# Score bounds as rows of the query tile, and gate logits as a column of the value projections

## The chip, the cores and the metric

The kernel runs on one core of a Trainium2 chip. Its five engines run their own instruction streams side by side: TensorE (PE, matrix products, with the weight loads shown apart as PEld), VectorE (DVE), ScalarE (ACT), GpSimd (POOL) and SyncE (SP, which here only issues DMAs). The metric is the device time of one execution in microseconds, as the median of several runs. The kernel before took 780.24 us, the median of three runs between 780.03 and 782.4.

## The reference

One layer of 2048 tokens by 512 features: attention with 32 heads of 16 features, a gated feed-forward network (FFN), and a sigmoid gate for each token that mixes the two. All arrays are bf16.

```python
x = A_x                                              # 1 x 2048 x 512
g = sigmoid((x * gate_w).sum(-1, keepdims=True))
q, k, v = split((x @ wqkv), 3, heads=32)             # Dh = 16
p = softmax(einsum("bhqd,bhkd->bhqk", q, k) * 16 ** -0.5)
a = concat_heads(p @ v) @ wo
b = (silu(x @ w_gate) * (x @ w_up)) @ w_down         # 512 -> 1792 -> 512
return g * a + (1 - g) * b
```

Softmax divides by a sum, so any number may be subtracted from a row's scores first. The kernel subtracts an upper bound of the row's scores instead of their maximum: for query q and head h, the sum over the 16 features d of |q_d| times the largest |k_d| of any key.

## The kernel before

**Tiling.** Queries go in four blocks of 512 (`qb`), heads in eight groups of four (`g`), keys in sixteen tiles of 128 (`kt`). A *unit* is a pair (qb, g); there are 32 of them, with group 0 of all four blocks first. A unit has sixteen *slots*, one for each key tile, so 512 slots in all, and every deadline in the code counts in slots. In a slot, PE makes the scores of four heads, 128 keys by 512 queries each; they are exponentiated, and PE multiplies them by the values (`vaug`, with a column of ones that gives the denominator) into the unit's `o_ps`.

**Layout of the score product.** A head has 32 partitions of the key tile `kaug` and of the query tiles `qx` and `q1`: the four heads of a group fill 128. In the kernel before, row 0 of the 32 is the bound (a one in `kaug`, minus the bound in the query tile), rows 1 to 16 the features, and the rest is zero in the query tile. `kaug` is filled with ones before the keys land. Some scores are made with 64 rows, two heads together; then the query tile's other plane holds zeros for the other head.

**Two ways to an exponential.** ACT exponentiates two heads' scores in one instruction (`e_t` from `s_t`, 128x1024, line 166), so a slot costs it two. Or DVE builds the slot: four conversions `c_t` from `d_t` (128x512 each, from PSUM, one for each head), which are the exponential's bits to first order, and then either three shifted copies of 128x2048 (`copy`, four approximations that the value product adds up, so that PE does four value products instead of one) or two bit operations and a product (`bits` and `product`, two value products). `kaug` and `wd_t` are used as homes for such tiles too, which is why the profile has rows like `kaug` from `d_t`.

**The planner.** All of this is ordered when the program is built. Every PE, ACT and DVE instruction goes out in the order in which the code calls it. `Plan` keeps an account of each engine's time: `spend` charges PE, `later(cost, f)` puts an instruction on a list for DVE with its cost, `ACT_US` is an exponential's cost and `MUL_US` that of the product in `product`. `v_unit` gives DVE a slot of the current or the next unit if DVE's account ends early enough before ACT would reach it; otherwise ACT gets it. Three PSUM banks (`m_tile`, `m_free`) serve projections, FFN products and `d_t`.

Side work is in chains (`pace.add(pieces, release, deadline, after, gap)`): projections, FFN products, output products. A chain starts at its release slot once the chains in `after` are done, and the one with the nearest deadline goes first. `need` forces chains at a slot; `q_of` says which chain must be done before DVE may take slots of a unit.

**The parts that the change touches.**

- `k_pieces` projects the keys of eight heads (b = 0 to 3) into `kst` and sends them to `kaug` by DMA. `k_bound` reduces |k| over all keys to `kb` (one number for each of 128 features), and multiplies a selection matrix `bsel` by it into `kneg` (128x8).
- `q_pieces` projects 512 queries of eight heads, copies them to `qst`, sends them to the query tiles in transfers of 16 rows, and puts |q| into `aq`.
- `bound_pieces` is a chain of its own: one product of `kneg` and `aq` into the bank `bp` (eight rows), an eviction to `bq`, four transfers into rows 0 of the query tiles. It follows `q_pieces` and `k_bound` with a gap of two slots.
- Group 0 has a path of its own (`q0_pieces`, `kneg0`), which stays as it is, with its bound in row 0.
- `v_pieces` projects the values of 128 keys for the 28 heads of groups 1 to 7: sixteen products of 128 by 448 columns (columns 64 to 511 of `wv`), evicted to `vaug`. Columns 0 to 63 (group 0) are read by `v0` and `v0_pieces` alone, earlier.
- `gate_pieces` makes the gate logits of two token tiles: eight products of one column each into `glog`, and a clamp to +-40 into `ge`. `gate_end` then makes the gate from all sixteen. `gw_col` is `gate_w` as a column, loaded in `late_loads` at slot 28.

SP issues every load and transfer in one queue in program order (the first small weights go through ACT's). GpSimd works in the first 11 us only.

Of the kernel before, what the change touches and what calls it, by code (L numbers as in the profile page):

```python
# [9 lines left out]
ALU = mybir.AluOpType  # L10
# [69 lines left out]
def kernel(  # L80
# [44 lines left out]
    SHIFTS = (25.0, 56.0, 94.0)  # L125
    EXP_A = 128.0 * inv_sqrt_dh * math.log2(math.e)
    EXP_B = {4: 128.0 * (127.0 - math.log2(5.372947814979324)), 2: 128.0 * (127.0 - math.log2(1.5015118813815151))}
    MUL_US = 1.2
    TINY = 1e-37
    AHEAD = 1  # L130
    SPARE = 0.5


# [28 lines left out]
    def mm(*args, **kw):  # L162
        return ordered(nc.tensor.matmul(*args, **kw))  # L163
# [42 lines left out]
    wo_l = big.tile([P, 2, D], BF16, name="wo_l")  # L206

    def late_loads():
        queue.dma_start(out=gw_col[:], in_=gate_w.rearrange("(dc p) -> p dc", p=P))
        queue.dma_start(out=wo_t[:], in_=A_wo.rearrange("(b p) d -> p b d", p=P))  # L210
        for i in range(2):
            for j in range(4):
                h = H - 8 + 4 * i + j
                queue.dma_start(out=wo_l[32 * j + 1:32 * j + 1 + DH, i, :], in_=A_wo[h * DH:(h + 1) * DH, :])
# [41 lines left out]
    for g in (1, 2):  # L256
# [9 lines left out]
    nc.gpsimd.memset(  # L266
        vaug[:, :, 0:G * 4 * VC].rearrange("p t (h c) -> p t h c", c=VC)[:, :, :, 0:1], 1.0)

    pidx = const.tile([P, 1], F32, name="pidx")
    nc.gpsimd.iota(pidx[:], pattern=[[0, 1]], base=0, channel_multiplier=1,  # L270
                   allow_small_or_imprecise_dtypes=True)
    bsel = const.tile([P, 8], BF16, name="bsel")
    lo_t = const.tile([P, 8], F32, name="lo_t")
    for h in range(8):
        c = 2 * (h % 4) + h // 4
        nc.gpsimd.memset(lo_t[:, c:c + 1], float(DH * h))
    far_t = const.tile([P, 8], F32, name="far_t")
    nc.gpsimd.memset(wo_l[:], 0.0)
    sbc_t = const.tile([P, P], BF16, name="sbc_t")
    nc.gpsimd.memset(sbc_t[:], 0.0)  # L280
# [6 lines left out]
        nc.gpsimd.memset(sel_t[32 * j:32 * j + 1, j:j + 1], 1.0)  # L287

    kb = const.tile([P, NB], F32, name="kb")
    kneg = const.tile([P, NB, 8], BF16, name="kneg")  # L290
    gval = const.tile([P, KT], F32, name="gval")
    omg = const.tile([P, KT], F32, name="omg")
    ge = const.tile([P, KT], F32, name="ge")
# [154 lines left out]
    def k_pieces(b, tb):  # L448

        def end(t, p):  # L450
            vec.tensor_copy(out=kst[b][:, t * QBW:(t + 1) * QBW], in_=p[:, :])
            m_free(p, plan.dve)
            if t == QB - 1:
                for hh in range(8):
                    g, j = 2 * b + hh // 4, hh % 4
                    if g > 0:
                        queue.dma_start(out=kaug[32 * j + 1:32 * j + 1 + DH, g, :],
                                          in_=kst[b][DH * hh:DH * (hh + 1), :])

        def lhs(dc):  # L460
            if dc == 0 and tb == 0:
                kst[b] = (on_t[1], bblk)[b == 1][:, :, :].rearrange("p b q -> p (b q)")
            return wqk[:, dc, D + P * b:D + P * (b + 1)]
        return columns(DC, "kp", lhs, lambda dc: xT[:, dc, tb * QBW:(tb + 1) * QBW],
                       lambda p: later(0.6, lambda: end(tb, p)))

    def k_bound(b):
        vec.tensor_reduce(out=kb[:, b:b + 1], in_=kst[b][:, :], axis=AX.X, op=ALU.max, apply_absolute_value=True)
        vec.tensor_scalar(out=kneg[:, b, :], in0=bsel[:, :], scalar1=kb[:, b:b + 1],
                          scalar2=None, op0=ALU.mult)  # L470

    def v0(t0):

# [33 lines left out]
    def v_pieces(tt):  # L507

        def end(p):
            dst = vaug[:, tt, 4 * VC:G * 4 * VC].rearrange("p (h c) -> p h c", c=VC)[:, :, 1:1 + DH]  # L510
            vec.tensor_copy(out=dst, in_=p[:, 64:D].rearrange("p (h c) -> p h c", c=DH))
            m_free(p, plan.dve)
        return columns(DC, "vp", lambda dc: xT[:, dc, tt * P:(tt + 1) * P], lambda dc: wv[:, dc, 64:D],
                       lambda p: later(0.54, lambda: end(p)), c0=64)

# [4 lines left out]
    for g in range(5, G):  # L522
# [1 line left out]

    q0 = [(qx[1][:, :, :, :], on_t[0][:, :, :].rearrange("p (v i) q -> p v i q", v=2))[qb // 2][:, :, qb % 2, :]
          for qb in range(QB)]
    aqs = {}

    def get_q(qb, g):
        return q1 if g == 1 else qx[(qb * (NB - 1) + g // 2 - 1) % 2][:, :, g % 2, :]  # L530
# [1 line left out]
    def q_pieces(qb, b):  # L532
        def landed(p):
            me = plan.chain
            later(0.6, lambda: end(p, me), key=("q", b))

        def end(p, me):
            qst = work.tile([P, QBW], BF16, tag="qst", name="qst")
            vec.tensor_copy(out=qst[:, :], in_=p[:, :])
            m_free(p, plan.dve)  # L540
            for hh in range(8):
                gg, j = hh // 4, hh % 4
                if (b, gg) != (0, 0):
                    queue.dma_start(out=get_q(qb, 2 * b + gg)[32 * j + 1:32 * j + 1 + DH, j % 2, :],
                                      in_=qst[DH * hh:DH * (hh + 1), :])

            def mag():
                aq = work.tile([P, QBW], BF16, tag="aq", name="aq", bufs=4)
                vec.tensor_scalar(out=aq[:, :].bitcast(U16), in0=qst[:, :].bitcast(U16),
                                  scalar1=0x7FFF, scalar2=None, op0=ALU.bitwise_and)  # L550
                aqs[(qb, b)] = aq
            plan.chain = me
            later(0.21, mag, plan.dve, ("q", b))
        return columns(DC, "qp", lambda dc: wqk[:, dc, P * b:P * (b + 1)],
                       lambda dc: xT[:, dc, qb * QBW:(qb + 1) * QBW], landed)
# [29 lines left out]
    def variants(p, to, q, more=()):  # L585
# [10 lines left out]
        later(0.4, select, key=key)  # L596
        for cost, f in more:
            later(cost, f, key=key)

    def bound_pieces(qb, b):  # L600

        st = {}

        def f():
            st["p"] = m_tile("bp")
            mm(st["p"][0:8, :], lhsT=kneg[:, b, :], rhs=aqs[(qb, b)][:, :], start=True, stop=True,
               tile_position=(0, 0))
            spend("C", 1)
            later(0.6, end)

        def end():
            bq = work.tile([8, QBW], BF16, tag="bq", name="bq")
            vec.tensor_copy(out=bq[:, :], in_=st["p"][0:8, :])
            m_free(st["p"], plan.dve)
            for j in range(4):
                if b == 0:
                    queue.dma_start(out=q1[32 * j:32 * j + 1, j % 2, :], in_=bq[2 * j + 1:2 * j + 2, :])
                else:
                    t = qx[(qb * (NB - 1) + b - 1) % 2]
                    queue.dma_start(out=t[32 * j:32 * j + 1, j % 2, :, :], in_=bq[2 * j:2 * j + 2, :])  # L620
        return [(1, f, True)]


    def gate_pieces(t0):
        def f():
            gp = m_tile("glog")
            for t in (t0, t0 + 1):
                for dc in range(DC):
                    mm(gp[:, t:t + 1], lhsT=xT[:, dc, t * P:(t + 1) * P],
                       rhs=gw_col[:, dc:dc + 1], start=(dc == 0), stop=(dc == DC - 1))  # L630
            spend("F", 2)

            def end():
                vec.tensor_scalar(out=ge[:, t0:t0 + 2], in0=gp[:, t0:t0 + 2], scalar1=-40.0, scalar2=40.0,
                                  op0=ALU.max, op1=ALU.min)
                m_free(gp, plan.dve)
            later(0.15, end)
        return [(0.7, f, True, "F", None)]

    def gate_end():  # L640
        act(out=ge[:, :], in_=ge[:, :], func=ACT.Exp, scale=-1.0)
# [507 lines left out]
    for g in (3, 4):  # L1149
        ones_rows(vec, g)  # L1150

    vec.tensor_scalar(out=lo_t[:], in0=lo_t[:], scalar1=pidx[:, 0:1], scalar2=None, op0=ALU.subtract)
    vec.tensor_scalar(out=far_t[:], in0=lo_t[:], scalar1=-float(DH) + 0.5, scalar2=-1.0,
                            op0=ALU.is_gt, op1=ALU.mult)
    vec.scalar_tensor_tensor(out=bsel[:, :], in0=lo_t[:], scalar=0.5, in1=far_t[:],
                                   op0=ALU.is_lt, op1=ALU.mult)
    plan.act = plan.pe
    plan.dve = plan.pe + 3.9

# [50 lines left out]
    need[9] = [v_late]  # L1210
    need[14] = [parts]
    q_of[0] = again
    v_rest = [pace.add(v_pieces(tt), 2, int(12 + 3 * tt)) for tt in range(KT)]

    def v_of(n):

# [12 lines left out]
    for qb in range(QB):  # L1229
        for b in range(NB):  # L1230
# [15 lines left out]
                rel = UNIT.index((qb - 1, 6)) * KT + 1 if qb else 0  # L1246
            else:
                rel = UNIT.index((qb, 2 * b - 2)) * KT + 1 if (qb, b) != (0, 2) else UNIT.index((0, 2)) * KT + 1
            q = pace.add(q_pieces(qb, b), rel, d - 25)
            bc = pace.add(bound_pieces(qb, b), rel, d - 22, [q] + after, 2)  # L1250
            need.setdefault(d - 12, []).append(bc)
            for g in {max(2 * b, 1), 2 * b + 1}:
                q_of[UNIT.index((qb, g))] = bc
    gates = [pace.add(gate_pieces(2 * i), 36 + 7 * i, 44 + 7 * i) for i in range(KT // 2)]
    gates = [pace.add([(0.2, gate_end, False)], 40, 106, gates)]
    turned = pace.add([(1, turn_odds, True, "F", None)], 40, 130, gates, 2)
    need.setdefault(160, []).append(turned)

# [118 lines left out]
    def begin(n):  # L1377
        plan.slot = n
        for c in need.get(n, []):
            force(c)  # L1380
        if n == 28:
            late_loads()
        i = n - (QB + 1) * KT - 8
        if 0 <= i < 2 * FC and i % 4 == 0:
            wd_load(i // 2)
        for f in at.pop(n, []):
            f()
        pace.begin_slot(n)
# [246 lines left out]
```

## Time and profile before

| what | value |
|---|---|
| median of three runs | 780.24 us |
| the profiled execution | 780.74 us |
| its span, first to last instruction | 778.8 us |
| granted TensorE clock, mean | 0.999 |
| first exponential starts, last one starts | 13.16 us, 769.69 us |
| `bq` from `bp`, 8x512, 16 times, DVE | 10.8 us busy, 673 ns each |
| `aq` from `qst`, 16 times, DVE | 4.6 us busy, 285 ns each |
| `ge` from `glog`, 8 times, DVE | 1.1 us busy, 151 ns each |
| `kneg` from `bsel` and `kb`, 4 times, DVE | 0.9 us busy, 229 ns each |
| `vaug` from `vp`, 128x448, 16 times, DVE | 9.9 us busy, 618 ns each |
| `bp`, 16 products, PE | 6.1 us busy, 379 ns each |
| `glog`, 64 products of one column, PE | 2.7 us busy, 165 ns each |
| loads and transfers | 32.63 MB, 42 GB/s over the span |

A group's *busy* time counts the time in which at least one of its instructions ran, and *mean* the duration of one. Instructions of one engine overlap (the next starts while the last results of the one before are still on their way), so a duration is longer than the step from one start to the next; where an engine is full, the step is the price. A timeline row merges neighbours of one kind: start, length, engine and line, operation, output and inputs, count, and in brackets the idle time before and what ended it. Since most instructions go through a helper, lines 163, 166 and 175 stand for nearly all of PE, ACT and DVE, and one reads by tile names.

### The profile page before, as it was taken

The page shows a single profiled execution, that of the slowest core. Times are in us where ns is not written, and L with a number is a line of the kernel's source. Part 1 is how long each engine was busy: PE and PEld are TensorE (multiplying, and loading weights), DVE is VectorE, ACT ScalarE, POOL GpSimd, SP SyncE. Part 2 cuts the span into 40 slices and gives each one's busy share as a digit, 9 for nine tenths or more (in the row PEclk, how much of TensorE's full clock was granted, in tenths as well). Part 3 has the DMA queues.
Part 4 walks back from the last instruction along what each step waited for, and adds up shares of the span by engine and source line. Part 5 has one row for each costly group of instructions (what it writes and reads, how often), then busy time and mean ns, then how long its engine had stood idle before and what let it go on. Part 6 is the DMA issues. An engine that isn't in the chain of part 4 may idle for free.

```text
span 778.8 us, 21608 instructions
## 1 busy us (share of the span) xinstructions
PE 740.7 (95%) x8877; PEld 223.6 (29%) x8877; DVE 725.5 (93%) x1162; ACT 764.5 (98%) x863; POOL 11.0 (1%) x34
## 2 busy tenths in 40 slices
PE   8999999999999999999999999989999989999997
PEld 3322333322222222232222222222222322222222
DVE  7799999899889999999999999999999999999994
ACT  5999999999999999999999999999999999999996
POOL 5000000000000000000000000000000000000000
PEclk9999999999999999999999999999999999999999
DMA  8002103134110112220100131211001222100001
GB/s 189 2 5 49 29 20 79 50 99 94 43 32 8 27 37 62 51 53 20 32 15 19 31 94 26 66 28 34 13 20 27 60 66 45 46 12 12 15 29 35
DMA packets 88138, 32.63 MB, mean 42 GB/s; under 512 B 74304, under 2 KB 87592, under 8 KB 88040
## 3 DMA queue, kind: packets, MB, share of 16 engines
q1 hardware_dynamic: 86312, 30.93, 16.5%
q8 instruction: 69, 1.13, 0.6%
q10 hardware_dynamic: 1728, 0.33, 0.2%
q14 instruction: 29, 0.24, 0.1%
HBM read 21.55 MB, written 2.35 MB: 31 GB/s over the span
## 4 chain that ended last, share of the span: by engine, by line
ACT 56%; PE 24%; issue 12%; DVE 7%; ACTq 0%; DVEq 0%
ACT e_t L166 53%; PE s_t L163 9%; PE o_ps L163 6%; PE gu L163 5%; DVE c_t L175 4%; ACT th L166 3%; PE qp L163 1%; PE dps L163 1%; DVE mt L175 1%; PE warm L163 1%; PE vp L163 1%; PE kp L163 1%; DVE gs L175 0%; PE ops L163 0%; DVE kaug L175 0%
## 5 line engine op out<-in xcount | busy, mean ns | idle before, releaser
L166 ACT ACTIVATE e_t<-s_t 128x1024 bf16<-128x1024 f32 x794 | 743.7, 1147 | 0.9 <-PE s_t L163 0.8
L175 DVE TENSOR_SCALAR c_t<-d_t 128x512 uint16<-128x512 f32 x404 | 267.8, 683 | 17.7 <-PE d_t L163 17.0
L163 PE MATMUL s_t<-qx,kaug 32*128 32x512 bf16 (+1 forms) x1252 | 244.3, 382 | 21.7 <-ACT e_t L166 19.6
L163 PEld LDWEIGHTS <-kaug 32*128 32x128 bf16 (+1 forms) x2048 | 97.9, 91 | 339.4 <-issue 334.6
L163 PE MATMUL o_ps<-e_t,vaug 128*32 128x512 bf16 x1588 | 154.9, 386 | 0.0
L175 DVE TENSOR_SCALAR c_t<-c_t 128x2048 uint16<-128x2048 uint16 x193 | 129.9, 685 | 1.1
L163 PE MATMUL d_t<-qx,kaug 32*128 32x512 bf16 x380 | 128.5, 384 | 0.0
L163 PE MATMUL o_ps<-c_t,vaug 128*32 128x512 bf16 x1028 | 97.8, 385 | 0.6 <-DVE osb L175 0.6
L163 PEld LDWEIGHTS <-vaug 128*32 128x32 bf16 x2800 | 59.5, 94 | 100.3 <-issue 94.2
L163 PE MATMUL gu<-xT,wg 128*32 128x512 bf16 x896 | 73.0, 384 | 0.0
L175 DVE TENSOR_TENSOR c_t<-c_t 128x2048 bf16<-128x2048 bf16 x59 | 71.7, 1215 | 0.0
L163 PE MATMUL gu<-xT,wu 128*32 128x512 bf16 x896 | 68.3, 382 | 0.1
L163 PE MATMUL ops<-wd_t,mt 128*32 128x512 bf16 x672 | 57.1, 382 | 0.0
L163 PE MATMUL s_t<-q,kaug 32*128 32x512 bf16 (+1 forms) x204 | 39.8, 382 | 6.0 <-ACT e_t L166 5.1
L175 DVE SCALAR_TENSOR_TENSOR gs<-th,gu 128x512 bf16<-128x512 bf16 x56 | 38.2, 682 | 3.4 <-ACT th L166 3.0
L175 DVE SCALAR_TENSOR_TENSOR mt<-gs,gu 128x512 bf16<-128x512 bf16 x56 | 38.2, 682 | 3.2 <-PE gu L163 1.5
L166 ACT ACTIVATE th<-gu 128x512 bf16<-128x512 f32 x56 | 40.9, 731 | 0.0
L175 DVE TENSOR_SCALAR kaug<-d_t 128x512 uint16<-128x512 f32 x52 | 34.8, 682 | 1.5 <-PE d_t L163 1.2
L163 PEld LDWEIGHTS <-mt 128*32 128x32 bf16 (+1 forms) x1037 | 24.1, 95 | 27.5 <-issue 21.6
L163 PEld LDWEIGHTS <-wu 128*32 128x32 bf16 x896 | 19.5, 95 | 24.1 <-issue 15.2
L163 PEld LDWEIGHTS <-wg 128*32 128x32 bf16 x896 | 17.4, 94 | 24.3 <-issue 21.8
L175 DVE TENSOR_SCALAR kaug<-c_t 128x2048 uint16<-128x2048 uint16 x35 | 24.0, 686 | 0.3
(149 smaller groups left out, 449.0 us busy)
## 6 DMA issues: line engine op xcount, KB each, us to landing
wg<-in_B_w_gate_dram SPq DMA_DIRECT2D x56, 128.0 KB
wu<-in_B_w_up_dram SPq DMA_DIRECT2D x56, 128.0 KB
on<-osb SPq DMA_DIRECT2D x120, 16.0 KB
rb<-rr SPq DMA_DIRECT2D x15, 128.0 KB
wd_t<-in_B_w_down_dram SPq DMA_DIRECT2D x7, 256.0 KB
qx<-qst SPq DMA_DIRECT2D x96, 16.0 KB
out_dram<-o_t SPq DMA_DIRECT2D x12, 128.0 KB
kaug<-on SPq DMA_DIRECT2D x20, 64.0 KB
```

The lines of the kernel that those rows point to most:

```text
L163: return ordered(nc.tensor.matmul(*args, **kw))
L166: ordered(nc.scalar.activation(*args, **kw))
L175: return lambda *a, **kw: ordered(f(*a, **kw))
```

## The change

The bound is no longer multiplied out. The query tile gets, beside the 16 rows of q, 16 rows of -|q_d| times `kb`, and `kaug` holds ones there, so that the score product itself adds the bound up. Rows 0 to 15 of a head are the features now and rows 16 to 31 the bound (group 0 keeps row 0). `aq` is q with its sign bit set, weighed by `kb` in place, and sent by the same transfers of 16 rows as q. `bound_pieces`, `bsel`, `lo_t`, `far_t`, `pidx` and `kneg` are gone; `q_pieces` waits for `k_bound` itself, and is due at `QLEAD` = 24 slots before use.

The gate vector is loaded at slot 3 and copied into column 63 of `wv`, which group 0's value products have read by then; each value projection takes 449 columns from column 63 on, and its first output column is the gate logit of its 128 tokens. `gate_pieces` is gone; the value projections wait for the copy, and their deadlines are two slots later. `MUL_US`, the planner's cost of the product, goes from 1.2 to 1.135.

```diff
-    MUL_US = 1.2
+    MUL_US = 1.135
+    QLEAD = 24
...
-        queue.dma_start(out=gw_col[:], in_=gate_w.rearrange("(dc p) -> p dc", p=P))
...
-                        queue.dma_start(out=kaug[32 * j + 1:32 * j + 1 + DH, g, :],
-                                          in_=kst[b][DH * hh:DH * (hh + 1), :])
+                        queue.dma_start(out=kaug[32 * j:32 * j + DH, g, :], in_=kst[b][DH * hh:DH * (hh + 1), :])
...
-        vec.tensor_scalar(out=kneg[:, b, :], in0=bsel[:, :], scalar1=kb[:, b:b + 1],
-                          scalar2=None, op0=ALU.mult)
...
         def end(p):
             dst = vaug[:, tt, 4 * VC:G * 4 * VC].rearrange("p (h c) -> p h c", c=VC)[:, :, 1:1 + DH]
+            vec.tensor_scalar(out=ge[:, tt:tt + 1], in0=p[:, 63:64], scalar1=-40.0, scalar2=40.0, op0=ALU.max, op1=ALU.min)
             vec.tensor_copy(out=dst, in_=p[:, 64:D].rearrange("p (h c) -> p h c", c=DH))
             m_free(p, plan.dve)
-        return columns(DC, "vp", lambda dc: xT[:, dc, tt * P:(tt + 1) * P], lambda dc: wv[:, dc, 64:D],
-                       lambda p: later(0.54, lambda: end(p)), c0=64)
+        return columns(DC, "vp", lambda dc: xT[:, dc, tt * P:(tt + 1) * P], lambda dc: wv[:, dc, 63:D],
+                       lambda p: later(0.69, lambda: end(p)), c0=63)
...
+        def rows(t, r):
+            for hh in range(8):
+                gg, j = hh // 4, hh % 4
+                if (b, gg) != (0, 0):
+                    queue.dma_start(out=get_q(qb, 2 * b + gg)[32 * j + r:32 * j + r + DH, j % 2, :],
+                                      in_=t[DH * hh:DH * (hh + 1), :])
...
+            rows(qst, 0)
+            aq = work.tile([P, QBW], BF16, tag="aq", name="aq")
             def mag():
-                aq = work.tile([P, QBW], BF16, tag="aq", name="aq", bufs=4)
-                vec.tensor_scalar(out=aq[:, :].bitcast(U16), in0=qst[:, :].bitcast(U16),
-                                  scalar1=0x7FFF, scalar2=None, op0=ALU.bitwise_and)
-                aqs[(qb, b)] = aq
+                vec.tensor_scalar(out=aq[:, :].bitcast(U16), in0=qst[:, :].bitcast(U16), scalar1=0x8000, scalar2=None,
+                                  op0=ALU.bitwise_or)
+                plan.chain = me
+                later(0.21, weigh, plan.dve, ("q", b))
+            def weigh():
+                vec.tensor_scalar(out=aq[:, :], in0=aq[:, :], scalar1=kb[:, b:b + 1], scalar2=None, op0=ALU.mult)
+                rows(aq, DH)
...
-    v_rest = [pace.add(v_pieces(tt), 2, int(12 + 3 * tt)) for tt in range(KT)]
+    def gate_column():
+        later(0.1, lambda: vec.tensor_copy(out=wv[:, :, 63:64], in_=gw_col[:].unsqueeze(2)))
+    gate_w_in = pace.add([(0.2, gate_column, False)], 9, 11, [v_late])
+    v_rest = [pace.add(v_pieces(tt), 2, int(14 + 3 * tt), [gate_w_in]) for tt in range(KT)]
...
-            q = pace.add(q_pieces(qb, b), rel, d - 25)
-            bc = pace.add(bound_pieces(qb, b), rel, d - 22, [q] + after, 2)
-            need.setdefault(d - 12, []).append(bc)
+            q = pace.add(q_pieces(qb, b), rel, d - QLEAD, after)
+            need.setdefault(d - 12, []).append(q)
             for g in {max(2 * b, 1), 2 * b + 1}:
-                q_of[UNIT.index((qb, g))] = bc
-    gates = [pace.add(gate_pieces(2 * i), 36 + 7 * i, 44 + 7 * i) for i in range(KT // 2)]
-    gates = [pace.add([(0.2, gate_end, False)], 40, 106, gates)]
+                q_of[UNIT.index((qb, g))] = q
+    gates = [pace.add([(0.2, gate_end, False)], 40, 106, v_rest)]
...
+        if n == 3:
+            queue.dma_start(out=gw_col[:], in_=gate_w.rearrange("(dc p) -> p dc", p=P))
```

The functions `bound_pieces` and `gate_pieces` are taken out whole, with the set-up of `bsel`.

More of the change, by code (lines that the diff above doesn't have):

```diff
@@ L267 @@
         vaug[:, :, 0:G * 4 * VC].rearrange("p t (h c) -> p t h c", c=VC)[:, :, :, 0:1], 1.0)
[L269 to L277, printed above, removed]
     nc.gpsimd.memset(wo_l[:], 0.0)
@@ L289 @@
     kb = const.tile([P, NB], F32, name="kb")
-    kneg = const.tile([P, NB, 8], BF16, name="kneg")
     gval = const.tile([P, KT], F32, name="gval")
@@ L526 @@
           for qb in range(QB)]
-    aqs = {}
     def get_q(qb, g):
@@ L540, in end @@
             m_free(p, plan.dve)
[L541 to L545, printed above, removed]
-            def mag():
-                aq = work.tile([P, QBW], BF16, tag="aq", name="aq", bufs=4)
-                vec.tensor_scalar(out=aq[:, :].bitcast(U16), in0=qst[:, :].bitcast(U16),
-                                  scalar1=0x7FFF, scalar2=None, op0=ALU.bitwise_and)
-                aqs[(qb, b)] = aq
+            rows(qst, 0)
+            aq = work.tile([P, QBW], BF16, tag="aq", name="aq")
+            def mag():
+                vec.tensor_scalar(out=aq[:, :].bitcast(U16), in0=qst[:, :].bitcast(U16), scalar1=0x8000, scalar2=None,
[5 more added lines that the diff above has]
+                rows(aq, DH)
             plan.chain = me
@@ L598, in variants @@
             later(cost, f, key=key)
[L600 to L638, printed above, removed]
     def gate_end():
@@ L1150 @@
         ones_rows(vec, g)
[L1152 to L1156, printed above, removed]
     plan.act = plan.pe
```

## The prediction

> **What bounds the kernel now.** I read four views: shares and groups of the page, the waits, ScalarE's (ACT's) timeline, and busy time by stretch.
>
> ```profile
> PE 740.7 (95%) x8877; PEld 223.6 (29%) x8877; DVE 725.5 (93%) x1162; ACT 764.5 (98%) x863; POOL 11.0 (1%) x34
> ...
> L166 ACT ACTIVATE e_t<-s_t 128x1024 bf16<-128x1024 f32 x794 | 743.7, 1147 | 0.9 <-PE s_t L163 0.8
> ```
>
> Three engines are above 90%, so shares alone don't choose. ACT's 794 exponentials (`e_t<-s_t`) are nearly all of its work, and it sat idle 0.9 us before them in the whole run. The waits have the same two neighbours from the other side:
>
> ```profile
> PE s_t L163 <- ACT e_t L166: 25.3, 77, 1.0
> DVE c_t L175 <- PE d_t L163: 17.0, 28, 1.3
> ...
> ACT e_t L166 <- PE s_t L163: 0.8, 2, 0.5
> ```
>
> TensorE (PE) waits for ACT 77 times, ACT for PE twice; VectorE (DVE) waits for scores to be made. Now ACT's timeline:
>
> ```profile
> 15.34 15.71 ACT L166 ACTIVATE e_t<-s_t 128x1024 bf16<-128x1024 f32 x17 [0.24 <-PE s_t L163]
> ...
> 700.58 70.16 ACT L166 ACTIVATE e_t<-s_t 128x1024 bf16<-128x1024 f32 x76
> 771.27 0.69 ACT L166 ACTIVATE osb<-o_ps,tiny 128x512 bf16<-128x512 f32 x1 [0.54 <-PE o_ps L163]
> ```
>
> The mean of 1147 ns is no price: exponentials overlap. From first start to last end, 76 take 70.16 us; less one duration (about 1.1) over 75 steps, that is 0.92 us each. The first 17 take 15.71 us, 0.91 each. The cadence hardly changes: from 15 us to 771 us the time is a count of ACT instructions times a fixed step.
>
> ```profile
> 40.00:765.00 725.00, 696.00 (x8409) 207.01 (x8403) 693.66 (x1085) 724.89 (x819) 0.00 (x0) 1.00 0.16 39
> ...
> 40.00:100.00 60.00, 58.98 (x719) 17.61 (x711) 59.31 (x95) 60.00 (x67) 0.00 (x0) 1.00 0.13 27
> 300.00:400.00 100.00, 95.41 (x1152) 28.74 (x1144) 96.47 (x153) 100.00 (x116) 0.00 (x0) 1.00 0.15 36
> 400.00:500.00 100.00, 95.94 (x1162) 28.40 (x1165) 98.19 (x155) 99.97 (x114) 0.00 (x0) 1.00 0.16 41
> ```
>
> Columns after the length: PE, weight loads, DVE, ACT, POOL. In the long middle ACT is busy 724.89 of 725 us, DVE 693.66 (95.7%). Where DVE reaches 98.2% or 98.9%, ACT still loses nothing. That decides below.
>
> **The change, part by part.** Score tiles are shared out when the program is built: ACT does a tile of four heads with two exponentials, or DVE builds it with bit arithmetic (four `d_t` conversions, then three shifted copies, or two bit operations and a product). The planner gives DVE a tile when its own account says that DVE has time. Counting instructions of the built program, ACT has 786 exponentials instead of 794: four more tiles on DVE (119 for 115), in five more of the three-copy form and one fewer of the product form. Prices are steps from start to start:
>
> ```profile
> 41.37 0.61 DVE L175 TENSOR_SCALAR on<-qst,vsel 128x512 bf16<-128x512 bf16 x2
> 41.90 0.62 DVE L175 CAST vaug<-vp 128x448 bf16<-128x448 f32 x1
> ...
> 89.61 1.22 DVE L175 TENSOR_TENSOR c_t<-c_t 128x2048 bf16<-128x2048 bf16 x1
> 90.74 0.15 DVE L175 TENSOR_SCALAR ge<-glog 128x2 f32<-128x2 f32 x1
> 90.81 0.74 DVE L175 TENSOR_SCALAR osb<-o_ps,tiny 128x512 bf16<-128x512 f32 x1
> ...
> 690.55 1.29 DVE L175 TENSOR_SCALAR c_t<-c_t 128x2048 uint16<-128x2048 uint16 x2
> 691.75 1.28 DVE L175 TENSOR_SCALAR c_t<-d_t 128x512 uint16<-128x512 f32 x2
> ...
> 693.71 0.68 DVE L175 CAST bq<-bp 8x512 bf16<-8x512 f32 x1
> 694.32 0.67 DVE L175 TENSOR_SCALAR c_t<-d_t 128x512 uint16<-128x512 f32 x1
> ```
>
> - *ACT*: 8 exponentials fewer, 8 x 0.92 = -7.4 us.
> - *DVE, bound*: 16 evictions `bq` go, 16 x 0.61 = -9.8. In comes the weighing, `aq` times `kb`, 16 times. No row multiplies `aq`; the nearest is `on<-qst,vsel`, the same shape and types with a column as the scalar: (41.90 - 41.37)/2 = 0.27, so +4.2. Bounds: 0.20 (the step of the sign operation on `aq`: +3.2) and 0.61 (an eviction: +9.8). `kneg` and the three set-up operations: -1.0.
> - *DVE, gate*: 8 clamps of two columns become 16 of one, 90.81 - 90.74 = 0.07 each: +0.6; between 0 and 16 x 0.15 - 0.6 = +1.8. One copy of the gate column: +0.1.
> - *DVE, the four tiles*: 16 conversions (0.60) +9.6, 13 copies and bit operations ((691.75 - 690.55)/2 = 0.60) +7.8, one product fewer (90.74 - 89.61) -1.1.
> - DVE's sum: -9.8 + 4.2 - 1.0 + 0.7 + 9.6 + 7.8 - 1.1 = **+10.4 us**, 9 to 17. It is covered by DVE's idle time: 725 - 693.7 = 31.3 us in the middle, of which 7.4 go with the shorter span. 704.1 busy of 717.6 is 98.1%, about what the stretch 400 to 500 shows with ACT undisturbed. Path cost 0; without cover it is the first rival.
> - *PE*: 16 products `bp` (0.22 behind another column product) -3.5, eight gate groups of 0.35 -2.8, 14 more value products of 0.22 +3.1, the 449th column nothing: -3.2 beside ACT, no time.
> - *`MUL_US` 1.2 to 1.135*: the product's step is 1.13, so the old account overstated 78 products by 0.065, 5.1 us in all. The new account is right; it also removes what had kept DVE ahead of its plan.
> - *DMA*: 112 transfers from `aq` replace 64 from `bq`, 48 more issues of about 0.58 us, 28 us of SP's time. Behind them on SP stand the FFN's weight loads, asked for two tiles ahead. A `qx` tile needs its 16 transfers (9.3 us to issue) and a landing; at most 4.7 us for that, the first weight load's time from issue at 0.8 us to ACT's use at 5.5 us. With 1.1 us on DVE that is 15 us. Between the last product of a query projection and the next unit's first score I find never fewer than 28 exponentials, 26 us: hidden, with 11 us to spare.
> - *Gate column*: `gate_w` (1 KB) is issued behind the projection weights, about 12.6 us; its copy stands on DVE behind the first `qst`, which was at 31 us, and behind it the selects of that query tile, all conversions after them, and PE's value projections, which read the column. Hidden unless the load takes 18 us.
>
> A rule of the Trainium skill gives another size. ScalarE: Activation LUTs, What ACT_TABLE_LOAD costs, has an activation at 186 ns plus 0.833 ns an element, with back-to-back ones overlapping by 93 ns: 946 ns per 1024 columns, an estimate of -7.6 us for eight. The trace's 0.92 decides.
>
> **The sum.** The profiled execution took 780.74 us, a span of 778.8 and 1.9 around it; 780.74 - 7.4 = 773.3. It lay 0.5 us above the median, 780.24, so I predict **773.0**.
>
> **Rivals.**
> *DVE becomes the bound* (slower). It needs 704.1 us of work in the middle. If it can't exceed the 96.5% of 300 to 400 us (it must wait for scores now and then), the middle lasts 729.9, +4.9: 785. Break-even is 704.1/725 = 97.1%, and the weighing at its upper bound adds 5.8 us. For it: DVE's idle time is partly 28 waits for PE, and no slack is left in the plan. Against: 98.2% over 100 us without loss to ACT. Chance 0.08.
> *The waits return as gaps* (same). DVE holds 97.1 to 97.4%; late `c_t` and held banks delay `s_t`, so each saved exponential comes back as gaps: 778 to 782, say 780. Chance 0.06.
> *The start loses some* (a smaller gain). Value projections now wait for the gate column, so the first wide key projection moves from 42.5 us to right behind the fourth exponential, near 18 us. Its weights were issued here:
>
> ```profile
> 11.56 1.05 SPq L175 DMA_DIRECT2D wqk<-in_A_wqkv_dram  x2
> ```
>
> DMA is 0.73 busy from 16 to 18 us and 0.01 after, so they are in by 18. If it is late by 2 to 3 us, PE stalls, then ACT: 775.5. Chance 0.08.
> *It doesn't do what it says*: were the freed time not used, 794 exponentials would stay and the time with them. The built program's count excludes it.
>
> **How the numbers follow.** Forecast 0.78, with 771 to 776 of its own; the smaller gain 0.08, same 0.06, slower 0.08. Measurement tells 0.3%, 2.3 us: faster is below 777.9. Faster 0.86, same 0.06, slower 0.08. Low end: ACT's steps at the first row's 0.91 would be worth several us more, but nothing in the change shortens them; I take 770.5. High end: the smaller gain and half of the same case, 779.
>
> **What will show it.** Right: 786 exponentials at 0.92, ACT full from 15 us to the end, DVE near 98% in the middle, `aq` weighed at about 0.27, no wait on the gate load. Wrong: `PE s_t` or `ACT e_t` waiting for DVE or DMA by several us, exponentials above 0.93, or a gap before 60 us.

## The result

The changed kernel took 777.55 us, the median of five runs (776.74 to 778.32), against 782.16 us for the kernel before in runs on the same chip (780.03 to 782.47). The ratio is 0.9955, with a 95% interval of 0.9944 to 0.9967; the two medians alone would give 0.9941, but the five runs of the kernel before lie in two groups, near 780.1 and 782.3 us, so their median is a poor base. It is faster, by 0.45%, inside the range on record, but by half of what was forecast (773.0 against 780.24 us is 0.93%).

### The profile page after: what moved, and what is told of

Same layout as the page of the kernel before. It is cut to its first block, busy times and chain, and to the rows that moved or that the text cites. A ratio compares the mean times of both kernels' runs of the same rounds, so it can differ in the third digit from the quotient of the medians.

```text
span 775.8 us, 21633 instructions
## 1 busy us (share of the span) xinstructions
PE 735.5 (95%) x8853; PEld 218.7 (28%) x8853; DVE 731.8 (94%) x1192; ACT 757.3 (98%) x855; POOL 10.6 (1%) x25
## 4 chain that ended last, share of the span: by engine, by line
ACT 41%; PE 28%; DVE 15%; issue 11%; DMA 2%; SPq 2%; DVEq 0%; ACTq 0%
ACT e_t L167 38%; PE s_t L164 10%; DVE c_t L176 10%; PE o_ps L164 7%; PE gu L164 3%; ACT th L167 2%; PE ops L164 2%; SPq L176 2%; PE qp L164 1%; PE kp L164 1%; DVE kaug L176 1%; DVE mt L176 1%; DVE gs L176 1%; DMA wg<-in_B_w_gate_dram 1%; PE vp L164 1%
## 5 line engine op out<-in xcount | busy, mean ns | idle before, releaser
L167 ACT ACTIVATE e_t<-s_t 128x1024 bf16<-128x1024 f32 x786 | 735.8, 1147 | 5.4 <-PE d_t L164 2.8
L176 DVE TENSOR_SCALAR c_t<-d_t 128x512 uint16<-128x512 f32 x396 | 262.1, 685 | 12.2 <-PE d_t L164 10.9
L164 PEld LDWEIGHTS <-kaug 32*128 32x128 bf16 (+1 forms) x2048 | 95.2, 91 | 339.7 <-issue 336.1
L164 PE MATMUL o_ps<-e_t,vaug 128*32 128x512 bf16 x1572 | 152.5, 386 | 0.1
L164 PE MATMUL d_t<-qx,kaug 32*128 32x512 bf16 x392 | 138.7, 385 | 0.0
L164 PE MATMUL o_ps<-c_t,vaug 128*32 128x512 bf16 x1096 | 102.1, 386 | 0.5 <-DVE osb L176 0.2
L164 PEld LDWEIGHTS <-vaug 128*32 128x32 bf16 (+1 forms) x2856 | 61.9, 94 | 99.9 <-issue 92.3
L176 DVE TENSOR_SCALAR kaug<-d_t 128x512 uint16<-128x512 f32 x72 | 48.0, 685 | 2.9 <-PE d_t L164 2.9
L176 DVE TENSOR_SCALAR c_t<-kaug 128x2048 uint16<-128x2048 uint16 x43 | 29.0, 687 | 0.1
```

What stands on the lines that cost most here:

```text
L167: ordered(nc.scalar.activation(*args, **kw))
L176: return lambda *a, **kw: ordered(f(*a, **kw))
```

## The profile after

First the shares of the page and its group of exponentials:

```profile
span 775.8 us, 21633 instructions
...
PE 735.5 (95%) x8853; PEld 218.7 (28%) x8853; DVE 731.8 (94%) x1192; ACT 757.3 (98%) x855; POOL 10.6 (1%) x25
...
L167 ACT ACTIVATE e_t<-s_t 128x1024 bf16<-128x1024 f32 x786 | 735.8, 1147 | 5.4 <-PE d_t L164 2.8
```

ACT's work fell as it was counted: 764.5 to 757.3 us, 7.2 us for eight exponentials. But the idle time in front of the exponentials rose from 0.9 to 5.4 us, and the span fell by 3.0 only. So the question is what ACT now waits for. The waits of the changed kernel, longest first:

```profile
PE s_t L164 <- ACT e_t L167: 25.1, 72, 0.8
DVE c_t L176 <- PE d_t L164: 10.9, 14, 2.0
...
PEld L164 <- DMA wg<-in_B_w_gate_dram: 4.4, 3, 2.3
...
PE gu L164 <- DMA wg<-in_B_w_gate_dram: 3.4, 2, 2.0
...
ACT e_t L167 <- PE d_t L164: 2.8, 2, 2.5
...
ACT e_t L167 <- PE s_t L164: 2.3, 4, 1.3
```

Two rows are new: PE waits for `wg`, the FFN's gate weights, to land. The kernel before had no such row. The largest of ACT's waits, 2.5 us, is in the stretch around 531 us. What SP issued before it, each row a merged group of DMA issues with start and length:

```profile
506.50 0.37 SPq L176 DMA_DIRECT2D wu<-in_B_w_up_dram  x1
516.52 0.55 SPq L176 DMA_DIRECT2D dd<-osb  x1
517.12 2.41 SPq L176 DMA_DIRECT2D on<-osb  x4
519.63 5.69 SPq L176 DMA_DIRECT2D qx<-qst  x8
525.41 4.97 SPq L176 DMA_DIRECT2D qx<-aq  x8
530.43 0.58 SPq L176 DMA_DIRECT2D wg<-in_B_w_gate_dram  x1
```

The next weight load goes out at 530.43, behind 13.9 us of small transfers, of which the eight from `aq` are 5.0. The kernel before had four from `bq` in this place, and the order of the queue was another:

```profile
509.29 0.37 SPq L175 DMA_DIRECT2D wg<-in_B_w_gate_dram  x1
...
527.60 2.50 SPq L175 DMA_DIRECT2D qx<-bq  x4
530.15 0.40 SPq L175 DMA_DIRECT2D wg<-in_B_w_gate_dram  x1
```

Counted in order, the load that is late in the changed kernel is the 42nd of 56; in the kernel before it went out at 509.29, ahead of the burst, and the one at 530.15 was wanted only at 603.6 us. So two things came together: the new order put this load behind the burst, and the burst is longer. Behind four transfers fewer it would have gone out near 527.9 (530.43 less the 2.5 us that four take) and landed 2.6 us later, as it did, near 530.5: an estimate, and just in time for PE, which wanted it at 531.04. PE's timeline in the changed kernel:

```profile
530.64 0.39 PE L164 MATMUL s_t<-qx,kaug 64*128 64x512 bf16 x2
533.04 1.27 PE L164 MATMUL gu<-xT,wg 128*32 128x512 bf16 x12 [2.00 <-DMA wg<-in_B_w_gate_dram]
534.23 0.61 PE L164 MATMUL s_t<-qx,kaug 32*128 32x512 bf16 x2
```

PE stands for 2.00 us until the load issued at 530.43 has landed; the next scores stand behind this product in PE's program and are made only at 534.23, and ACT runs dry. After the wait the products are slow as well: twelve take 1.27 us where 0.83 is usual, a score pair 0.61 where 0.39 is. Busy time in single microseconds, with the granted clock as the first number after POOL:

```profile
531.00:532.00 1.00, 0.04 (x2) 0.00 (x0) 1.00 (x3) 1.00 (x2) 0.00 (x0) 1.00 0.20 48
532.00:533.00 1.00, 0.00 (x0) 0.00 (x0) 0.94 (x1) 0.43 (x1) 0.00 (x0) 1.00 0.97 221
533.00:534.00 1.00, 0.96 (x12) 0.25 (x12) 0.00 (x0) 0.00 (x0) 0.00 (x0) 0.65 1.04 235
534.00:535.00 1.00, 1.00 (x11) 0.25 (x11) 0.08 (x1) 0.06 (x1) 0.00 (x0) 0.50 1.03 232
535.00:536.00 1.00, 1.00 (x10) 0.10 (x2) 0.61 (x1) 1.00 (x2) 0.00 (x0) 0.50 0.31 71
```

PE's idle time of 2 us is followed by a clock of 0.50 to 0.65 until nearly 537 us. The hole at 115 us goes with a wait of 1.38 us for `wg`, also behind sixteen transfers, but the clock stays at 1.00 there. From one exponential's start to the next the two places cost 2.8 and 1.5 us beyond the usual 0.90.

## The experiments

All ratios are to the kernel before, run on the same chip. Theory 1 is that the shortfall is the weight loads' place in SP's queue. Rival A is that DVE is too full to keep its plan. Rival B is that the DMA engines are late, not the queue.

**A fourth weight buffer.** The order of PE, DVE and ACT is unchanged.

```diff
-    ffnw = ctx.enter_context(tc.tile_pool(name="ffnw", bufs=3))
+    ffnw = ctx.enter_context(tc.tile_pool(name="ffnw", bufs=4))
...
+                    w_load(2, True)
+                    w_load(2, False)
-                w_load(i + 2, True)
-                w_load(i + 2, False)
+                w_load(i + 3, True)
+                w_load(i + 3, False)
```

> The kernel after, with a fourth buffer for the FFN weights, asked for three tiles ahead instead of two; the order of PE, DVE and ACT is the same instruction for instruction. Theory 1 (the weight loads come late because they stand in SP's queue behind a burst of 16 query-tile transfers): PE's wait for wg, 3.4 us + 4.4 us in the waits of after, goes, both holes of ACT (1.5 us at 115 us, 2.8 us at 531 us) go, ratio to before near 0.990. Rival A (DVE is too full): holes stay or move, ratio stays at 0.9955. Rival B (the DMA engines, not the queue, are late): a load that is issued earlier also helps here, ratio 0.990 to 0.994; the next run tells it from theory 1.

773.99 us, ratio 0.9913 (0.99 to 0.9925). The hole at 531 us is gone. The one at 115 us shrinks only, from 1.5 to 1.1 us: the FFN's first loads are asked for when its first tile begins, whatever the number of buffers, and still went out at 113.37 us behind sixteen transfers:

```profile
ACT e_t L167 <- PE s_t L164: 1.9, 4, 0.9
...
PE gu L164 <- DMA wg<-in_B_w_gate_dram: 1.0, 1, 1.0
```

DVE's instructions and their order are the same, so its fullness didn't make the hole: rival A falls for it. I had expected both holes to go, and the second shows why only one did.

**The transfers from `aq` on GpSimd's queue.**

```diff
-        def rows(t, r):
+        def rows(t, r, by=queue):
...
-                    queue.dma_start(out=get_q(qb, 2 * b + gg)[32 * j + r:32 * j + r + DH, j % 2, :],
+                    by.dma_start(out=get_q(qb, 2 * b + gg)[32 * j + r:32 * j + r + DH, j % 2, :],
...
-                rows(aq, DH)
+                rows(aq, DH, Ordered(nc.gpsimd))
```

> The kernel after, with the 112 transfers from aq issued by GpSimd instead of SP; nothing else moves. Theory 1: the burst on SP is 8 transfers shorter (about 5 us) and the weights come 5 us earlier: at 531 us the wait of 2.0 us goes, at 115 us the wait of 1.4 us goes, ratio near 0.990. Rival A: 0.9955. Rival B (bandwidth or the DMA engines): the same bytes move at the same time, so the waits stay, 0.9955. If GpSimd's issue is slow, the bound rows land later, and PE's s_t or d_t would wait for a DMA.

773.51 us, ratio 0.9908 (0.9894 to 0.9922). The same bytes go to the same places by another engine's queue, and the wait for `wg` is gone from the waits. SP's issues near the place of the old hole:

```profile
518.33 5.84 SPq L176 DMA_DIRECT2D qx<-qst  x8
524.21 0.58 SPq L176 DMA_DIRECT2D wg<-in_B_w_gate_dram  x1
```

and the group of exponentials:

```profile
L167 ACT ACTIVATE e_t<-s_t 128x1024 bf16<-128x1024 f32 x786 | 735.3, 1145 | 1.3 <-PE s_t L164 1.1
```

The weight load goes out 6.2 us earlier in the run (4.9 us if both are counted from the start of the burst), and the idle time before the exponentials is down to 1.3 us, from 5.4. Rival B falls, since the transfers didn't get fewer.

**The planner's account alone**, on the kernel before.

```diff
-    MUL_US = 1.2
+    MUL_US = 1.135
```

> The kernel before with the planner's product cost 1.135 alone: 792 exponentials for 794. If an honest account costs nothing: 2 x 0.92 = 1.8 us less, ratio 0.9976. Rival A (the overstated cost was a needed reserve): ratio 1.000 or above, with more waits for c_t or d_t.

780.77 us, ratio 1.0006 (0.9998 to 1.0015): 792 exponentials and no gain. The end of ACT's timeline shows where it went:

```profile
699.48 69.03 ACT L166 ACTIVATE e_t<-s_t 128x1024 bf16<-128x1024 f32 x75
770.84 0.69 ACT L166 ACTIVATE osb<-o_ps,tiny 128x512 bf16<-128x512 f32 x1 [2.33 <-PE o_ps L163]
```

The exponentials keep their step, but the last unit's output waits 2.33 us for its last value products, where the kernel before waited 0.54. The 1.8 us are given back at the tail. The trace shows by whom: DVE finishes a last tile from 767.19 to 770.35 us, PE's last value products start when it is done, at 770.40, and the output follows them. In the kernel before DVE had no tile there; its last value products multiplied an exponential of ACT. So the account seems to have given DVE a slot too near the end.

**The old account with the rest of the change.**

```diff
-    MUL_US = 1.135
+    MUL_US = 1.2
```

> The kernel after with the product cost back at 1.2: 788 exponentials. Theory 1: 6 x 0.92 = 5.5 us less than before, plus whatever hole the bursts of this order make in front of a weight load: ratio 0.993 without a hole, 0.996 with one of 2 to 3 us, and the hole again stands at a wg wait. Rival A: the reserve is back, so no holes, and the ratio is better than that of after, 0.993 or less, with DVE waits for PE back at 17 us.

777.16 us, ratio 0.9965 (0.9952 to 0.9979): 788 exponentials, and holes again, one of 1.8 us at 110 us with a wait of 1.77 us for `wg` beside it, and one of 1.2 us at 115 us, in a stretch at a clock of 0.50 that follows this wait. The reserve in the account does not protect from them. A later hole, 1.4 us from 333 to 336 us, has no late load, against the expectation; it follows 1 us of PE waiting for ACT, and the clock:

```profile
330.00:331.00 1.00, 0.00 (x1) 0.02 (x1) 1.00 (x3) 1.00 (x3) 0.00 (x0) 1.00 0.00 0
331.00:332.00 1.00, 0.80 (x10) 0.36 (x9) 1.00 (x2) 1.00 (x2) 0.00 (x0) 1.00 0.00 0
332.00:333.00 1.00, 1.00 (x10) 0.16 (x9) 1.00 (x3) 1.00 (x2) 0.00 (x0) 0.53 0.00 0
```

The profiled execution took 779.39 us at a mean clock of 0.994; eight of the twelve took 776.34 to 777.49 at 0.999 or 1.000, so in most of them the clock cost less than it does in this trace.

**The gate part alone**, on the kernel before: the load at slot 3, `gate_column`, the 449 columns, the clamps and the later deadlines of the diff; all else as before.

> The kernel before with the gate part alone (load at slot 3, column 63 of the value projections, one clamp for each token tile, deadlines two slots later), cost 1.2, bounds as before: 794 exponentials, as before. Theory 1: no exponential is saved and no transfer is added, so nothing to gain or lose: ratio 0.999 to 1.001, no wait for a weight load above 0.5 us. Rival (the moved start costs something, the third rival of the prediction): a gap of ACT before 60 us and a ratio up to 1.003.

781.16 us, ratio 1.0005 (0.9997 to 1.0014), 794 exponentials, and no wait for a weight load. It neither gains nor loses.

**The bound part alone**: the kernel after with the gate part undone and the account at 1.2.

> The kernel before with the bound part alone, cost 1.2, gate as before: 794 exponentials, as before, so ACT saves nothing. Theory 1: the longer bursts of 16 transfers are there, and where FFN weights are wanted behind one, PE waits for wg: ratio 1.000 to 1.006, each hole in ACT with a wg wait beside it. Rival A (fullness of DVE makes the holes): DVE has less work here than before (the evictions of bq are gone), so no hole, ratio at or below 1.000.

787.63 us, ratio **1.0086** (1.0065 to 1.0108): alone, the bound makes the kernel slower, by more than I had allowed. The waits, and SP's queue in front of the worst of them:

```profile
PEld L164 <- DMA wg<-in_B_w_gate_dram: 7.1, 3, 4.2
ACT e_t L167 <- PE s_t L164: 7.0, 6, 3.9
...
PE gu L164 <- DMA wg<-in_B_w_gate_dram: 5.9, 3, 3.7
```

```profile
313.10 5.92 SPq L176 DMA_DIRECT2D qx<-qst  x8
319.11 4.97 SPq L176 DMA_DIRECT2D qx<-aq  x8
324.18 1.85 SPq L176 DMA_DIRECT2D wg<-in_B_w_gate_dram  x1
```

The same picture as at 531 us, worse: PE stands for 3.7 us, ACT for 3.9, and the clock is at 0.50 from 328 to 334 us. DVE is emptier here (721.0 us busy) than before (725.5), so fullness can't be the cause.

**The bound part alone, `aq` on GpSimd's queue** (the two edits together).

> The bound part alone, cost 1.2, with the transfers from aq on GpSimd's queue: 794 exponentials in the same order as in the run of the bound part alone (1.0086). Theory 1: the holes go with the long bursts, ratio 0.998 to 1.001, no wg wait above 0.5 us. If the bound rows themselves were late (query tiles not landed when their unit begins), or DVE's new weighing cost something on the path, part of the 0.86% would stay.

781.57 us, ratio 1.0010 (1.0001 to 1.0019). Of the 0.86%, 0.76 go with the queue, and no wait for `wg` is left. The rest, 0.7 us, is less than the 0.3% that a comparison tells.

**The other queue with other accounts.** First 1.2:

> The transfers from aq on GpSimd's queue, and the product cost at 1.2: 788 exponentials. Without holes 6 x 0.92 = 5.5 us less than before: ratio 0.993. Against the run with 1.135 on the same queue (786, 0.9908) it shows what the account is worth without the queue: 1.8 us if an honest account costs nothing; if the reserve is worth something, the two are equal.

775.57 us, ratio 0.993 (0.9917 to 0.9943), 788 exponentials: the count, to the third digit. Against 0.9908 with 1.135, the account is worth 0.22% here, 1.7 us for two exponentials; on this queue it isn't lost at the tail. Then 1.03, below the product's own step:

```diff
-    MUL_US = 1.135
+    MUL_US = 1.03
```

> The transfers from aq on GpSimd's queue, and the product cost at 1.03, 0.10 below its measured step: 784 exponentials. If ACT's count sets the time alone: 10 x 0.92 = 9.2 us less than before, ratio 0.988. Rival A (DVE becomes the bound once it is told to do more than it can): DVE falls behind its plan, PE waits for c_t and for banks, ACT's steps grow, and the ratio is 0.991 or above.

771.75 us, ratio **0.9882** (0.9869 to 0.9896), 784 exponentials: the count again. DVE isn't at its limit yet. The middle of this run:

```profile
40.00:755.00 715.00, 687.42 (x8344) 204.90 (x8337) 699.62 (x1118) 714.81 (x808) 64.91 (x112) 1.00 0.18 42
```

DVE is busy 699.62 of 715 us, 97.8%, and ACT loses 0.2.

**Both cures at once**, the other queue and the fourth buffer, with the account at 1.03.

> The transfers from aq on GpSimd's queue, product cost 1.03 (784 exponentials), and a fourth buffer for the FFN weights as well. Theory 1: with no weight wait left, the fourth buffer adds nothing: ratio 0.988, as without it. If shorter weight waits were still hidden in ACT's steps, it would be 0.987 or less.

772.09 us, ratio 0.9885 (0.9872 to 0.9899): no different from the run without the fourth buffer. Nothing was left for it to cure. The fastest version found is the one before: the change, `aq` on GpSimd's queue, and the account at 1.03.

## Why the prediction was half right

- *ACT sets the time, and eight exponentials fewer are worth 7.4 us*: right in kind and size. ACT's busy time fell by 7.2 us, and with the queue cured the kernel took 0.9908 of the time before, which is 7.2 us of 780.24. Over the four versions with `aq` on the other queue, 794, 788, 786 and 784 exponentials gave 1.0010, 0.993, 0.9908 and 0.9882 (the first without the gate part).
- *DMA, "hidden, with 11 us to spare"*: this is the step that failed. It named the FFN's weight loads as what stands behind the transfers on SP, and then priced the arrival of the query tiles, which was indeed never late. Nothing was worked out for the loads. Two tiles ahead was taken for a reserve of time, but the loads are issued by the FFN's own progress, and a burst between two issues can use all of it up: 13.9 us at 531 us. Paired in order, every load of `wg` in the kernel before was issued at least 5.9 us ahead of its tile's first product; in the changed kernel four were not more than 3.9 us ahead, PE's waits included, and the one at 531 us took 2.6 us to land; in the five runs with `aq` on the other queue the least is 5.3. The term left out was about 4 us: 1.5 and 2.8 us of holes, part of the second by the slowed clock. The sixteen issues themselves were priced too low as well: 9.3 us, where they took 10.0 at 103 us and 10.8 at 520 us.
- *DVE takes the work into its idle time*: right in kind, too high in size. Its busy time rose by 6.3 us where the steps gave 10.4, and in the middle it was busy 699.39 of 722 us, 96.9%, not 98.1. Added up group by group the busy times rose by 13.0 us, so neighbours overlap more than before; that fewer gaps part them is the likely reason. The weighing's step is 0.26 us (687.99 to 688.25 us in the timeline), forecast 0.27. DVE's wait for PE's scores (`c_t` from `d_t`) fell from 17.0 to 10.9 us. The rival that made DVE the bound didn't come, even at 784.
- *PE -3.2 us, no path*: busy time fell by 5.2.
- *The start*: the first wide key projection ran at 16.6 us, and the gate column was copied at 31.98 us with no wait. The gate part alone is worth nothing either way, and the smaller gain came from another place than that rival named.
- *The account*: I called it right and therefore free. Alone it bought two exponentials and lost them at the tail (1.0006); after the change, with `aq` on the other queue, it was worth its two.

## What to carry to other kernels

When a change adds small transfers to a queue, price each thing behind them and not only what they carry: how long the queue is blocked at its longest, against how far ahead the next load is asked for. If the engine in front takes its work in order, one late load stops everything that stands behind it, even work that needs nothing of it. And a change in two parts can hide that one of them alone loses: here the bound alone cost 0.86%. Nor do the gains of parts add up: each part alone left the planner at 794 exponentials, both together at 788, and the account made it 786.

## What was not expected of the hardware

A short stop of PE can cost more than its length. After 2.0 us without a product (531 to 533 us) the granted clock went to 0.65 and 0.50 until nearly 537 us. In the run of the old account it fell to 0.50 twice, after the stop of 1.8 us at 110 us and after one of 1.0 us (330 to 331 us, then 0.53 and 0.50 from 332 us). After the stop of 1.4 us at 115 us it stayed at 1.00. The Trainium skill, TensorE: Matmul & The Clock Gate, What's actually happening, puts half speed after at least one idle window of about 3.4 us, in windows that run freely. The half speed agrees with the 0.50 here, but the stops that these traces show are shorter than that, so a reserve of 3.4 us is not safe here.

Why one stop of 1.0 us slowed PE and one of 1.4 us didn't, the traces answer in part. The slow phases last 3.41 us (533.29 to 536.70 us in the changed kernel, 113.60 to 117.02 and 332.06 to 335.47 with the old account) or twice that (327.54 to 334.36, the bound part alone), and the two of the old account begin 218.45 us apart, which is 64 such phases. So the clock seems to be decided anew in fixed steps of 3.41 us. In the step right before these four falls PE was idle for 2.00, 1.71, 1.45 and 3.07 us. The stop at 115 us lies whole in one step, 113.45 to 116.86 us counted back from 533.29, with 1.38 us idle. So the idle time that falls into one step goes with the fall, and a stop at 330 us can count more than a longer one, because shorter gaps in the same step add to it. This is read off four falls and was not tried; idle time alone can't be the whole measure, since at 764 us the run of both cures had 1.9 us of it in one step and kept its clock.

One program does not lose the clock in every execution. Of the five of the changed kernel two had a mean clock of 1.000 and took 776.74 and 776.85 us; the other three, with the profiled one, had 0.998 and took 777.55 to 778.32. So a lost clock seems worth about 1 us here.
